# One add in place of two accumulations: spectral products of a long convolution summed on VectorE and GpSimd instead of TensorE

## The chip, the cores and the metric

The kernel runs on one core of a Trainium2 chip. The metric is the device time of one execution in microseconds; of several runs the median is given. A core has five engines that work side by side, each through its own list of instructions in order: TensorE (PE in the profile, its weight loads PEld) for matmuls, VectorE (DVE), ScalarE (ACT), GpSimd (POOL), and SyncE (SP), which here issues all DMAs. Matmul results land in PSUM, eight banks of 128x512 f32; all else lives in SBUF.

## The reference

All inputs are bf16; S is 2048 positions, D is 512 channels, F is 1792.

```python
# A: long convolution with a gate, on qn = layernorm(q)
k_shift = sum over 4 taps of shifted k * shift_k        # short causal convolution
kv      = k_shift * v
y       = irfft(rfft(pad(kv)) * rfft(pad(ssm_k)))[:S]   # causal convolution over all 2048 positions
h       = q + qn * (y + kv * ssm_D)
# B: a block with two layernorm stages, on x = layernorm(h)
g       = gelu(layernorm(x) @ w1), its four channel quarters shifted by +1, -1, +2, -2 positions
x1      = x + g @ w2
out     = h + x1 + gelu(layernorm(x1) @ w3) @ w4
```

## The kernel before, in words

**Halves and blocks.** The positions are cut into two halves, s = 0 and 1, of 8 blocks b of 128 rows; pairs p of blocks go together through the block's matmuls. The convolution is made by transforms that are written as matmuls in two steps. A signal's first step is S1 (`step1`, line 389) and its copy out of PSUM E1; eight DMAs X (line 405) then reorder it between partitions; the second step is S2 (line 413) with its copy E2. There are four signals: F0 and F1, the two halves of the filter, and A0 and A1, the two halves of kv. For F1, E2 isn't a copy but a fold: VectorE adds and subtracts F0's spectrum (line 425). kv itself comes from K (matmuls with diagonal matrices of the taps, line 442) and KV (VectorE multiplies by v, line 450). The diagonal matrices, one per channel group c, are made by `dg`, lines 296 to 309, on VectorE as four scalings of an identity or on GpSimd as one select.

**The products and the way back**, `conv(s, prods)`, from line 465. For each k of 0 to 3 (`kl`) a spectral product P(s, k, i, x) is one VectorE multiply of 128x2048 bf16 (line 474); i counts the pairs of signals, x the two forms of a complex product. Then I2(s, k, .), 16 matmuls (line 484), takes a product back one step; EV copies the four banks out, XI sends them through a DMA, and I1 (line 502) is the last step back. The first half has one pair of signals, A0 with F0: two products and two I2 for each k. The second half has two pairs, A0 with F1 and A1 with F0: four products and four I2 for each k, all accumulating in the same four banks.

**Behind it.** H (line 616) makes h from I1's banks, with the normalized q (Y, lines 611 and 613, from the statistics Q, QV, QP, QN of q), HS its statistics, uw, rr, hn the factors, hb the normalized block, LT and TE its transposition, W and U the matmul with w1 and its gelu, X2 (line 722) the matmul with w2, S (line 725) the sum x1, R a sum for the end, SS, ux, r1, xn, lb, LX, EX the same for the second layernorm, M and G (lines 777 and 781) the matmul with w3 and its gelu, O (line 790) the matmul with w4, Z the last sum, OUT the store. Some block pairs are transposed by two DMA writes and one DMA transpose, the others on TensorE; the list `BYDMA` says which.

**What sets the order.** Every step is entered with `plan.add`: a name, the engines that it may run on with a cost for each, what it depends on, and the buffers that it takes and drops. The string `ORDER` then gives the whole schedule: each word has a step's number, the letter of its engine (P, V, A, G, S for SyncE; M for two joined ScalarE copies) and the numbers of the slots that it takes, PSUM banks among them. The steps are emitted in this order, so it fixes each engine's list. An engine waits where a step's input or slot isn't ready, and everything behind it in that list waits too. Products take two of eight slots in `prs`.

In the order before, the second half's convolution stands among the first half's W, X2, M and O: I2 of k = 0 behind W of the last pair, k = 1 behind M of pair 1, k = 2 and 3 among M of pair 0, then O.0.1, O.0.0 and I1 of the second half. Here X.s.b stands for step X of half s and block b, P.1.k.i.x for a product of the second half.

Of the kernel before, what the change touches and what calls it, by code (L numbers as in the profile page):

```python
# [9 lines left out]
P = 128  # L10
# [21 lines left out]
004S 029P0 000S 002S 003S 005S 008S 031V 037V 001S 030P 063P23 006S 055P45 009S 057P67 064V 007S 056A 038G 065P01 010S 058A 019S 059P45 033V 045G  # L32
061P23 060A 087P60 039G 036V 062A 095P71 046V 042V 066A 093P4 032G 043V 047A 074S 101P5 044A 034G 015S 094V 051P23 022S 088V 053P01 035G 023S 052A
040V 072S 089P4 024S 054A 049G 091P6 021S 090V 073S 041A 097P2 096V 050G 070S 092V 099P3 048A 069S 102V 068S 107P01 098V 109P67 017S 100V 108A 103P45
067S 110V 111P23 018S 104A 115P01 071S 113P67 112A 323V 105P45 324V 116A 211P20 106V 114A 117P01 212V 119S 118A 084P4567 326V 085A 081P2301 123S 329V
086V 120S 083A 215P4 020S 082A 330V 124S 078P0167 327V 125S 217P5 080A 216V 121S 079A 075P2367 012S 218V 011S 325V 076A 127P4501 016S 319V 328V 122S
077A 219P21 129V 126S 331G 128A 013S 220V 130P6701 139V01 132A 141V23 131A 133P4501 332G 134A 140P23670 147V45 142P 135A 333G 149V67 143A 337G0
148P45011 155V01 150P 343G1 144A 145S 221P2 340G2 157V23 152A 146S 334G3 014S 151A 136P6701 222V 137V 138A 156P23452 153S 158P 154S 163V45 225P0 159A
223P1 160A 165V67 161S 164P67230 162S 226V 166P 224V 175P45 167A 168V 213P0 176A 169S 183P67 214V 170S 185P23 184A 187P45 315S 186V 177P01 188A 189P67
178V 179P23 190A 181P45 180V 171P67 028S 182A 172P01 338V 192S 231P45 196S 335V 339A 349G0 173P23 316S 344V 336A 346G3 193S 341V 235P67 232A 355G1  # L40
195S 347V 174P10 236A 352G2 191S 350V 237P45 198S 358G 342A 356V 202P6723 197S 348A 353V 194S 345A 359G 204V 239P01 238A 371G 203V 241P23 240A 227P45
242A 229P01 372G 360V 228V 230A 199P6723 247S 361G0 373V 233P45 351A 364G1 200V 362P00 234A 374G2 365P1 384V 366A 377G3 208P6745 245S 363V 354A 375P11
243S 201V 385G 367P0 376A 244S 357A 378P1 386V 246S 369P2 379A 390V0 318S 209V 397G 387A1 382P3 248S 370A 250S 388P12 210V 368A 398G 391P6 249S 380P7
383A 389A 027S 392V 399G 251P2345 263V01 381A 393P0 253A 026S 400G3 265V23 395P1 025S 252A 317S 403V2 205P6745 396A 267V45 401P23 394A 404P3 502P1
402A 206V 405A 506P0 503V 408P2 507V 504A 406P3 269V67 508A 409A 264P67011 558V 407A 266P 207V 268P 559G 270P 560G 498P2 271A 272V 561G1 510P3 564G0
499V 274S 494P4 501V 273S 562P50 511V 565P6 514P7 563A 495V 566A 411V 254P0123 496A 567P50 515V 256A 275V01 569P4 568A 577P6 277V23 570A 257P2345 578A
412V 573P7 259A 255V 571P6 258A 279V45 579P4 572A 574A 281V67 575P5 580A 516A 276P01232 414V 500A 278P 513V 280P 576A 615G 512V 282P 581P6 505V 283A
616G 517V 284A 617G 413V 621G3 287V01 618A2 619P71 587G 622P4 582V 260P0123 620V 583S 584P5 623V 588G 262A 289V23 589G 291V45 591A1 590G0 293V67
624P40 593S 261V 636P6 592S 625A 634P7 416V 509V 288P23010 635A 594S2 290P 299V01 292P 285S 294P 301V23 628P4 296A 632P7 303V45 629A 298S 637A 626P0
286S 633A 305V67 630P1 295A 410V 627A 297S 300P67231 417V 631A 302P 415V 304P 306P 418V 641P4 307A 419G 308A 309S 310S 420V 421V0 427G3 638P0 424G1  # L50
430V2 585V 642V 497V 311P16 639V 312P72 640S 422V 643S 313P35 425V 423A 433G0 428V 314P40 426A 431V 439A3 595P10 445G 442V1 432A 603P2 436V2 429A 437V
597P6 596A 434V 446G 605P7 598A 438A 447V 599P1 448V2 435A 451G3 322V 458V 607P5 600A 470V 459G 449P33 452P6 601P1 450V 453A 471G 460V 604A 440V 454P6
602A 472G 441V 461A2 456P3 443V 474G1 462A3 444V 473G0 608A 476S 606A 612P2 482V 475S 457A 463S 483G 464S 609P1 484V 477S0 485A1 486G0 455A 487S 321V
488S 465S1 518P0 522P3 489S2 480P4 523V 478P5 519V 524A 468P3 520A 481A 466P7 644V 521V 645G 490P6 467A 525V 646G 469A 492P0 610V 320G 479A 647V2
534P3 491A 648V3 649S 493A 650S 542P4 535V 554P5 537V 536A 538P3 651S3 555V 546P7 543V 556A 586S 545V 526P1 544A 611S 539V 530P6 547V 540A 550P3 527V
672G 652P00 529V 531V 658P1 673G 528V 656P5 659A 674V 532V 653A 675G1 662P4 657A 549V 676G0 660P7 551V 678S 654P5 552V 661A 677S 664P3 553V 655A 756G
548A 533V 663A 679S0 700V 665A 666P6 701G 702V 703V3 704G2 613V 669P7 757G 667V 706S 705S 541V 758G 557V 759G0 728G 680P10 729G 686P0 681A 730V 731V1
682P5 732G2 670V 687A 688P4 684P3 707S1 760G3 689A 692P2 668S 761S 693A 733S 685A 734S 708P60 714P4 735S2 712P1 720P0 671S 713A 762S 710P2 721A 715A
716P3 711A 736P10 683A 763S3 717A 742P0 709A 614S 737A 748P6 743A 738P4 749A 764P50 772P7 776P6 774P2 777A 765A 766P3 775A 768P6 767A 773A 744P5 769A
740P1 770P0 741A 739A 771A 778P2 718P4 779V 780S 719A 725P3 722P4 726V 727S 781P7 723V 724S 690P4 782V 783S 691A 697P6 745A 694P7 746P1 695V 698V 696S  # L60
747A 750P0 699S 753P2 751V 752S 754V 755S
# [32 lines left out]
def body(ctx, tc, fx, kt, q, v, sd, w1, w2, w3, w4, out):  # L94
# [200 lines left out]
    def dg(c):  # L295
        def f(e, sl):
            if e == GP:
                tap = r_k[:, c * KW + NB * 129:(c + 1) * KW].rearrange("p (j x) -> p j x", x=2)[:, :, 1:2]
                pool.affine_select(out=diag[:, c], in_=tap.to_broadcast([P, 4, P]), compare_op=OP.is_equal, fill=0.0, base=0,
                                   pattern=[[0, 4], [-1, P]], channel_multiplier=1)  # L300
                return
            for j in range(4):
                sc = r_k[:, c * KW + NB * 129:(c + 1) * KW].rearrange("p (o x) -> p o x", o=1)[:, 0, :].bitcast(F32)[:, j:j + 1]
                if e == A:
                    act.activation(diag[:, c, j, :], ident[:], ACT.Copy, scale=sc)
                else:
                    vec.tensor_scalar(out=diag[:, c, j, :], in0=ident[:], scalar1=sc, scalar2=None, op0=MUL)  # L307
# [155 lines left out]
    last_p = []  # L463

    def conv(s, prods):
        for kl in range(4):
            n = ("I2", s, kl, 0)
            for i, (a, g) in enumerate(prods):
                for x in range(2):
                    before = last_p[-1:]  # L470

# [7 lines left out]
                    def f(e, sl, i=i, x=x, kl=kl, n=n, first=first, last=last):  # L479
                        bk = got(n)  # L480
                        for xx in range(2):
                            for t in range(2):
                                for h in range(4):
                                    nc.tensor.matmul(ps[64 * t:64 * t + 64, bk[h], :], lhsT=ttab[32 * h:32 * h + 32, 2 * kl + t, 2 if x else xx, :],  # L484
                                                     rhs=prs[32 * h:32 * h + 32, got(("P", s, kl, i, x))[t], xx, :],
                                                     start=first and xx == 0, stop=last and xx == 1)
                    add(("I2", s, kl, 2 * i + x), {PEc: 0.44}, f,
                        ["tt"] + [("E2", y, kl, t) for ag in prods for y in ag for t in range(2)] if first else [("I2", s, kl, 2 * i + x - 1)],
                        take=[("ps", -2), ("vs", 1)] if first else [], drop=[(("P", s, kl, i, x), 0)], mode=3)
            for hp in range(2):  # L490
                add(("EV", s, kl, hp), EV, lambda e, sl, hp=hp, n=n: copy(e, vst[:, got(n, "vs")[0], 2 * hp:2 * hp + wide(e), :], pair(got(n), hp, wide(e))),
                    [("I2", s, kl, 2 * len(prods) - 1)], drop=[(n, hp)], mate=None if hp else (("EV", s, kl, 1), n, 0, n, 2))
# [12 lines left out]
    def qstat(s, b):  # L505
        return lambda e, sl: vec.bn_stats(qst[:, 8 * s + b, :], q_sb[:, s, b, :])
# [337 lines left out]
```

## Time and profile before

| | us |
|---|---|
| median of 3 runs | 214.38 (212.96 to 215.33) |
| the profiled execution | 213.26 |
| its span | 211.6 |
| TensorE busy | 195.7 |
| VectorE busy | 144.8 |
| ScalarE busy | 125.5 |
| GpSimd busy | 80.1 |
| VectorE, 24 spectral products (line 474) | 28.7, 1.24 each |
| TensorE, 384 matmuls of I2 (line 484) | 13.3 |
| 16 DMAs of XI, each to landing (median) | 3.9 |

The span is that of the instructions in the profile; the execution's time has 1.7 us more around it. Durations of neighbouring instructions overlap a little in the listing, so where many of one kind follow each other, the distance from start to start is the better price (six products in 7.12 us, so 1.19). A busy engine isn't yet the bound: the page gives its share in 40 slices of the span, and the chain that ended last tells where it was waited for. The granted clock of TensorE is 1.0 throughout.

### The profile page before, as it was taken

Reading aid. Unit: us, or ns where it says so; the run is one execution under the profiler, and the core shown is the slowest. Engines: PE = TensorE matmul, PEld = TensorE weight load, DVE = VectorE, ACT = ScalarE, POOL = GpSimd, SP = SyncE. Lnnn points to the kernel's source line nnn. Section 1 sums busy time; section 2 is a strip of 40 time slices with the busy share of each in tenths; the row PEclk is TensorE's granted clock in tenths of the full one; section 3 lists DMA queues with packets and bytes.
Section 4 is the critical chain, followed back from the end, with each engine's and each line's share of the span. In section 5 each row is a group of like instructions: output and inputs, shape, how many; then the busy total and the mean of one; then the engine's idle time right before and its main releaser. Section 6 shows DMA issues by size and latency. Waiting matters only on the chain.

```text
span 211.6 us, 5040 instructions
## 1 busy us (share of the span) xinstructions
PE 195.7 (93%) x1964; PEld 116.2 (55%) x1980; DVE 144.8 (68%) x302; ACT 125.5 (59%) x206; POOL 80.1 (38%) x177
## 2 busy tenths in 40 slices
PE   6899769898889999979999999989999999999992
PEld 5454323442248546636744884645848888645450
DVE  6998999999999999999868971559972000112031
ACT  3979989787999658943751883364623565301010
POOL 7850059804888140287044683212765000000000
PEclk9999999999999999999999999999999999999999
DMA  6999895976948995000693008533146440010011
GB/s 173 313 403 397 321 325 222 256 205 237 371 169 294 332 435 147 0 28 13 89 232 92 27 22 181 98 69 82 42 107 154 102 74 0 3 50 34 16 50 50
DMA packets 30809, 32.86 MB, mean 155 GB/s; under 512 B 20545, under 2 KB 22594, under 8 KB 30530
## 3 DMA queue, kind: packets, MB, share of 16 engines
q1 hardware_dynamic: 30786, 32.55, 50.8%
q8 instruction: 15, 0.25, 0.5%
q14 instruction: 8, 0.07, 0.1%
HBM read 13.14 MB, written 4.46 MB: 83 GB/s over the span
## 4 chain that ended last, share of the span: by engine, by line
PE 59%; DVE 13%; ACT 12%; DMA 6%; issue 3%; POOL 3%; SPq 3%; DVEq 0%; ACTq 0%; POOLq 0%
PE ps L777 21%; PE ps L790 18%; ACT r_a L257 5%; PE ps L722 5%; PE ps L699 5%; PE ps L484 3%; DVE r_v L616 3%; DMA r_dg<-dhb 2%; DMA r_a<-r_a 2%; PE ps L502 2%; PE ps L413 2%; DMA r_k<-in_kt_dram 2%; DVE r_f L425 2%; DVE r_dg L307 1%; DVE r_p L474 1%
## 5 line engine op out<-in xcount | busy, mean ns | idle before, releaser
L777 PEld LDWEIGHTS <-r_k 128*128 128x128 bf16 x448 | 43.5, 98 | 7.7 <-issue 1.2
L792 DVE TENSOR_TENSOR r_v<-ps,r_v 128x512 bf16<-128x512 f32 x16 | 10.7, 686 | 42.4 <-PE ps L790 42.4
L474 DVE TENSOR_TENSOR r_p<-r_a,r_f 128x2048 bf16<-128x2048 bf16 x24 | 28.7, 1240 | 1.0 <-PE ps L484 0.6
L777 PE MATMUL ps<-r_dg,r_k 128*128 128x256 bf16 x224 | 25.6, 273 | 0.1
L257 ACT CAST r_a<-ps 128x1024 bf16<-128x1024 f32 x23 | 22.2, 1026 | 3.0 <-PE ps L413 2.8
L781 ACT ACTIVATE r_f<-ps 128x512 bf16<-128x512 f32 x14 | 7.8, 599 | 20.6 <-PE ps L777 20.6
L613 POOL TENSOR_SCALAR z_t<-r_q,qrs,qnm 128x512 f32<-128x512 bf16 x11 | 13.0, 1188 | 12.6 <-DVE r_v L616 12.0
L442 PE MATMUL ps<-r_dg,r_k 128*128 128x256 bf16 (+3 forms) x108 | 15.2, 284 | 1.6 <-ACT r_f L257 0.8
L257 ACT CAST r_vs<-ps 128x1024 bf16<-128x1024 f32 x14 | 13.7, 1032 | 4.9 <-PE ps L484 4.9
L725 DVE SCALAR_TENSOR_TENSOR r_q<-r_v,hrr,ps 128x512 bf16<-128x512 bf16 x16 | 11.4, 742 | 5.9 <-PE ps L722 3.7
L781 ACT ACTIVATE r_a<-ps 128x512 bf16<-128x512 f32 x14 | 7.8, 606 | 12.2 <-PE ps L777 12.2
L257 ACT CAST r_f<-ps 128x1024 bf16<-128x1024 f32 x14 | 13.2, 1023 | 3.0 <-PE ps L389 2.8
L442 PEld LDWEIGHTS <-r_k 128*128 128x128 bf16 x112 | 9.5, 98 | 9.5 <-issue 4.8
L484 PE MATMUL ps<-r_p,ttab 32*64 32x512 bf16 x384 | 13.3, 379 | 1.0 <-DVE r_p L474 0.8
L699 PEld LDWEIGHTS <-r_fx 128*128 128x128 bf16 x128 | 12.3, 98 | 3.2 <-DMA r_dg<-dhb 0.6
L600 ACT ACTIVATE junk<-r_v 128x512 bf16<-128x512 bf16 x14 | 8.9, 635 | 7.3 <-DVE r_v L616 7.1
L777 PE MATMUL ps<-xtx,r_k 128*128 128x256 bf16 x112 | 13.0, 273 | 0.0
L600 ACT ACTIVATE junk<-r_q 128x512 bf16<-128x512 bf16 x12 | 7.6, 630 | 9.2 <-DVE r_q L725 9.1
L777 PE MATMUL ps<-xty,r_k 128*128 128x256 bf16 x112 | 12.7, 272 | 0.0
L790 PE MATMUL ps<-w4s,r_f 128*128 128x512 bf16 x54 | 12.5, 379 | 0.1
L748 POOL TENSOR_TENSOR xrr<-xrr,mhalf 128x2 f32<-128x2 f32 x8 | 7.2, 900 | 14.2 <-DVE xrr L745 13.8
L389 PEld LDWEIGHTS <-f 128*32 128x32 bf16 x256 | 6.1, 95 | 11.3 <-issue 7.5
(183 smaller groups left out, 374.7 us busy)
## 6 DMA issues: line engine op xcount, KB each, us to landing
r_z<-r_vs SPq DMA_DIRECT2D x16, 256.0 KB, 3.9
r_k<-in_kt_dram SPq DMA_DIRECT2D x8, 260.0 KB, 4.6
r_v<-in_v_dram SPq DMA_DIRECT2D x4, 512.0 KB, 7.3
r_f<-r_f SPq DMA_DIRECT2D x8, 256.0 KB, 5.2
r_q<-in_q_dram SPq DMA_DIRECT2D x8, 256.0 KB, 5.7
r_a<-r_a SPq DMA_DIRECT2D x8, 256.0 KB, 4.2
r_f<-r_a SPq DMA_DIRECT2D x8, 256.0 KB, 4.2
r_a<-r_z SPq DMA_DIRECT2D x8, 256.0 KB, 4.1
```

What stands on the lines that cost most here:

```text
L257: (act.copy if e in "AM" else on[e].tensor_copy)(o, i)
L442: nc.tensor.matmul(o[:, (d + j0) * P:(d + j1 + 1) * P], lhsT=kT[s][c][:, bb, x:x + P], rhs=diag[:, c, j0:j1 + 1, :].rearrange("p j x -> p ...
L474: on[e].tensor_tensor(out=prs[:, sl[0]:sl[0] + 2, :, :], in0=sp[a][:, kl, :, :, :], in1=gv, op=MUL)
L484: nc.tensor.matmul(ps[64 * t:64 * t + 64, bk[h], :], lhsT=ttab[32 * h:32 * h + 32, 2 * kl + t, 2 if x else xx, :], rhs=prs[32 * h:32 * h + ...
L600: act.activation(junk[:], x, ACT.Square, accum_out=sq[:, i, 1:2])
L613: on[e].tensor_scalar(out=z_t[:, sl[0], :], in0=qs, scalar1=qrs[:, i:i + 1], scalar2=qnm[:, i:i + 1], op0=MUL, op1=ADD)
L699: nc.tensor.matmul(ps[:, sl[0], j * 256:(j + 1) * 256], lhsT=w1s[:, k, m * P:(m + 1) * P], rhs=xt[:, k, :], start=(k == 0), stop=(k == DC ...
L725: vec.scalar_tensor_tensor(out=q_sb[:, s, b, :], in0=h_sb[s][:, b, :], scalar=hrr[:, 4 * s + b // 2, 0, b % 2:b % 2 + 1], in1=ps[:, got((" ...
L777: nc.tensor.matmul(ps[:, sl[0], j * 256:(j + 1) * 256], lhsT=w3s[:, k, fc * P:(fc + 1) * P], rhs=xt[:, k, :], start=(k == 0), stop=(k == D ...
L781: act.activation(gb[:, 2 * fp:2 * fp + 2, :], ps[:, got(("M", s, p, fp))[0], :].rearrange("p (j x) -> p j x", j=2), ACT.Gelu_apprx_tanh)
L790: nc.tensor.matmul(ps[:, sl[0], :], lhsT=gb[:, fc, (b % 2) * P:(b % 2 + 1) * P], rhs=w4s[:, fc, :], start=(fc == 0), stop=(fc == FC - 1))
L792: add(("Z", s, b), {V: 0.61}, lambda e, sl, b=b: vec.tensor_tensor(out=h_sb[s][:, b, :], in0=ps[:, got(("O", s, b))[0], :], in1=h_sb[s][:, ...
```

## The change

It has five parts.

1. **Sums of products.** In the second half, for each k and x, the two products (i = 0 and 1) are added elementwise by a new step PA, in place in the slots of the first product, on VectorE or GpSimd. I2 is then run on the sum alone: two I2 of 16 matmuls for each k in place of four. The first half is as before. A product no longer waits for the product entered before it.
2. **Diagonals.** `dg` has only its GpSimd form.
3. **Statistics of q.** For blocks 4 to 7 of the second half, Q moves from VectorE to ScalarE: two passes with a sum each, of q and of its square; QV has three more small instructions to bring both forms together.
4. **A new order** of all steps, with other engines for some of them. Of the eight adds, PA.1.0.0, PA.1.2.0 and PA.1.3.0 are on GpSimd, the other five on VectorE. All four `dg` are on GpSimd (two before); f2v and dr, GpSimd's before, are on VectorE; QV of the second half goes from VectorE to GpSimd.
5. `BYDMA` stays: the same block pairs are transposed by DMA.

Some stretches of the new order around the adds, engine by engine:

```
VectorE  P.1.0.0.1 P.1.0.0.0 P.1.0.1.1 P.1.0.1.0 E2.F1.2.1 S.0.2 S.0.3 PA.1.0.1 P.1.1.0.0 E2.F1.2.0 S.0.1 S.0.5 SS.0.5 EX.0.3
         S.0.0 S.0.4 P.1.1.0.1 P.1.2.0.0 R.0.4 R.0.1 P.1.1.1.1 PA.1.1.1 P.1.1.1.0 PA.1.1.0 P.1.2.1.1 EX.0.0 Q.1.1 Q.1.0
         P.1.2.0.1 P.1.2.1.0 R.0.2 lb.0.4 lb.0.5 Q.1.2 E2.A1.3.0 PA.1.2.1 P.1.3.1.0 P.1.3.0.0 P.1.3.1.1 P.1.3.0.1 PA.1.3.1 Q.1.3
GpSimd   hb.0.6 hb.0.7 PA.1.0.0 ux.0.1 r1.0.1 xn.0.1 lb.0.2 ux.0.0 r1.0.0 xn.0.0 lb.0.0 lb.0.1 ux.0.2 r1.0.2 xn.0.2
         PA.1.2.0 PA.1.3.0 edge1 QV.1 QP.1 Y.1.2
TensorE  S2.F1.2 LT.0.7 X2.0.2 X2.0.3 W.0.3.0 W.0.3.1 I2.1.0.0 I2.1.0.1 X2.0.1 X2.0.5 X2.0.4 LX.0.2 LX.0.3 X2.0.0 S2.A1.1
         six M of pair 1, S2.A1.2 M.0.1.6 O.0.2 LX.0.0 LX.0.1 I2.1.1.0 I2.1.1.1 O.0.3 S2.A1.3 six M of pair 0
         I2.1.2.0 I2.1.2.1 M.0.0.5 O.0.1 I2.1.3.0 I2.1.3.1 O.0.0 M.0.2.0 M.0.2.1 M.0.2.2 I1.1.0
```

The diff without the order and without the lines that only make room for a new block:

```diff
@@ dg @@
-            if e == GP:
-                tap = ...
-                pool.affine_select(out=diag[:, c], ...)
-                return
-            for j in range(4):
...
+            tap = ...
+            pool.affine_select(out=diag[:, c], ...)
-        add(("dg", c), {V: 0.8, A: 1.19, GP: 0.85}, dg(c), [("Lk", 0, c)], port="VG")
+        add(("dg", c), {GP: 0.65}, dg(c), [("Lk", 0, c)], port="VG")
@@ conv @@
-                    add(("P", s, kl, i, x), {V: 1.15}, f, [("E2", y, kl, t) for y in (a, g) for t in range(2)] + ["f2"] + before, take=[("pr", -1)], port="VG")
-                    last_p.append(("P", s, kl, i, x))
-                    first, last = (i, x) == (0, 0), (i, x) == (len(prods) - 1, 1)
+                    add(("P", s, kl, i, x), {V: 1.15}, f, [("E2", y, kl, t) for y in (a, g) for t in range(2)] + ["f2", "tt"], take=[("pr", -1)], port="VG")
+                    first, last, y = x == 0, x == 1, ("P", s, kl, 0, x)
+                    if i < len(prods) - 1:
+                        continue
+                    if i:
+                        def f(e, sl, x=x, kl=kl):
+                            pa, pb = (prs[:, got(("P", s, kl, j, x))[0]:got(("P", s, kl, j, x))[0] + 2, :, :] for j in range(2))
+                            on[e].tensor_tensor(out=pa, in0=pa, in1=pb, op=ADD)
+                        add(("PA", s, kl, x), {V: 1.135, GP: 3.0}, f, [y, ("P", s, kl, i, x)], drop=[(("P", s, kl, i, x), 0)], port="VG")
+                        y = ("PA", s, kl, x)
...
-                                                     rhs=prs[32 * h:32 * h + 32, got(("P", s, kl, i, x))[t], xx, :],
+                                                     rhs=prs[32 * h:32 * h + 32, got(("P", s, kl, 0, x))[t], xx, :],
...
-                    add(("I2", s, kl, 2 * i + x), {PEc: 0.44}, f,
-                        ["tt"] + [("E2", y, kl, t) for ag in prods for y in ag for t in range(2)] if first else [("I2", s, kl, 2 * i + x - 1)],
-                        take=[("ps", -2), ("vs", 1)] if first else [], drop=[(("P", s, kl, i, x), 0)], mode=3)
+                    add(("I2", s, kl, x), {PEc: 0.44}, f, [y] if first else [y, ("I2", s, kl, 0)],
+                        take=[("ps", -2), ("vs", 1)] if first else [], drop=[(("P", s, kl, 0, x), 0)], mode=3)
@@ qstat @@
+        if s == 0 or b < 4:
+            return lambda e, sl: vec.bn_stats(qst[:, 8 * s + b, :], q_sb[:, s, b, :])
+        def f(e, sl):
+            act.activation(junk[:], q_sb[:, s, b, :], ACT.Identity, accum_out=qst[:, 8 * s + b, 0:1])
+            act.activation(junk[:], q_sb[:, s, b, :], ACT.Square, accum_out=qst[:, 8 * s + b, 1:2])
+        return f
@@ qvar @@
+            if s:
+                j = slice(12, 16)
+                en.tensor_scalar(out=qmv[:, j, 0], in0=qst[:, j, 0], scalar1=1.0 / D, scalar2=0.0, op0=MUL, op1=ADD)
+                en.tensor_tensor(out=qrs[:, j], in0=qmv[:, j, 0], in1=qst[:, j, 0], op=MUL)
+                en.tensor_tensor(out=qsd[:, j], in0=qst[:, j, 1], in1=qrs[:, j], op=SUB)
+                i = slice(8, 16)
@@ steps of q @@
-            add(("Q", s, b), {V: 0.6}, qstat(s, b), [("Lq", s, b // 2)])
+            add(("Q", s, b), {A: 1.3} if s and b > 3 else {V: 0.6}, qstat(s, b), [("Lq", s, b // 2)])
```

More of the change, by code (lines that the diff above doesn't have):

```diff
@@ L505, in qstat @@
     def qstat(s, b):
-        return lambda e, sl: vec.bn_stats(qst[:, 8 * s + b, :], q_sb[:, s, b, :])
+        if s == 0 or b < 4:
[4 more added lines that the diff above has]
+        return f
     def qvar(s):
-        i = slice(8 * s, 8 * s + 8)
         def f(e, sl):
             en = on[e]
+            i = slice(8 * s, 8 * s + (4 if s else 8))
             m0, v0, m1, v1 = (qst[:, i, k] for k in (1, 2, 4, 5))
```

77 lines of the change are left out of this document (35 added, 42 removed).

## The prediction

> **What bounds the kernel now.** I read the page's first two parts, then the chain that ended last, then the timelines of single engines. The page says that TensorE (PE) is nearly always busy, that its clock is never lowered, and that VectorE (DVE) is full too until slice 20, at 106 us:
>
> ```profile
> PE 195.7 (93%) x1964; PEld 116.2 (55%) x1980; DVE 144.8 (68%) x302; ACT 125.5 (59%) x206; POOL 80.1 (38%) x177
> PE   6899769898889999979999999989999999999992
> DVE  6998999999999999999868971559972000112031
> PEclk9999999999999999999999999999999999999999
> ```
>
> The chain, in order of time, splits the span. Up to 48.5 us it changes hands between DMA, VectorE and ScalarE. From 62 to 208 us it is TensorE almost without a break, and the steps that the change shortens (L484, the step back I2 of the second half) lie on it, 64 matmuls at a time:
>
> ```profile
> 73.80 1.86 PE ps L484 x64
> 100.39 1.86 PE ps L484 x64
> 102.26 3.60 PE ps L777 x32
> 105.86 1.87 PE ps L484 x64
> 113.92 3.61 PE ps L502 x16
> ```
>
> So between the first I1 (L502, 48.50) and the last I2 (ends 107.73) two engines are full side by side. I summed the steps of each engine's list over this stretch, by start-to-start spacings from the timelines. On TensorE: S1 0.485, I1 0.945, transposes of a block 0.22, W 0.875, S2 0.57, X2 0.87, I2 0.467, M 0.89, O 3.0. This gives 53.0 us of work in 59.2, so 6.2 us of gaps and waits, most of it before 62 us. On VectorE: H, S and R 0.67, folds E2 of F1 1.2, casts 1.13, product P 1.16, Q 0.60, HS and SS 0.85. From the first H (49.66) to the last P (ends 105.67) it is 54.3 us of work in 56.0, 1.7 us of waits. VectorE has no more room than TensorE.
>
> **Part 1, fewer matmuls.** Each k of the second half has four I2 steps of 16 matmuls, 1.86 us; two remain. Gone: 4 x 0.93 = 3.7 us, all on the path above. This is the whole possible gain of the edit itself.
>
> **Part 2, the adds on VectorE.** Five of the eight adds (PA) run there. An add has the shape and type of P, so 1.16 each, 5.8 us. My list for the new order, first H to last add, has 54.0 us against 54.3: the five adds, three statistics instead of one (1.7), a Y, two lb and one more copy of a transposed block (9.0 in all) stand against three casts, two Q, two R, two hb, Z, uw, ux and two hn gone (9.3). VectorE is no lighter while TensorE is lighter by 3.7 us: it becomes the bound of this stretch.
>
> **Part 3, the adds on GpSimd.** PA.1.0.0, PA.1.2.0 and PA.1.3.0 go there, 128x2048 bf16 with two inputs. No row shows that. From below: a one-input 128x512 op takes 0.757 us undisturbed (four in 3.03), so 3.0 for four times the size. Two-input rows: f2 with 256 elements 0.61, dr with 512 elements 1.21. With 0.195 for the smallest op as fixed part they give 3.55 and 4.27; f2 scaled without it gives 4.9, the upper end. I take 4.0, between the two nearest rows.
>
> The second price is that the two engines hold each other up:
>
> ```profile
> 34.31 3.73 POOL L613 TENSOR_SCALAR z_t<-r_q,qrs,qnm 128x512 f32<-128x512 bf16 x1
> 32.92 4.63 DVE L474 TENSOR_TENSOR r_p<-r_a,r_f 128x2048 bf16<-128x2048 bf16 x4
> 50.52 3.03 POOL L613 TENSOR_SCALAR z_t<-r_q,qrs,qnm 128x512 f32<-128x512 bf16 x4 [9.15 <-DVE r_v L616]
> 66.81 2.84 POOL L655 TENSOR_SCALAR nbx<-r_v,hrr,hnm 128x512 bf16<-128x512 bf16 x1
> 69.01 0.79 DVE L655 TENSOR_SCALAR nbx<-r_v,hrr,hnm 128x512 bf16<-128x512 bf16 x1
> ```
>
> The same GpSimd step takes 0.757 beside VectorE's H (which reads PSUM) and 3.73 beside a run of products, ending half a microsecond after that run; the products keep their 1.16. At 69.01 it is VectorE that waits: its step takes 0.79, not the 0.41 of its like, until GpSimd's of 66.81 ends. So whoever is in first goes through, and a GpSimd add delays VectorE's products and adds, but not its steps that read PSUM.
>
> [...]
>
> With times counted from the first I1, and 4.0 + 0.1 per GpSimd add:
> - PA.1.0.0: VectorE ends P.1.0.1.0 at 1.16 + 20.7 + 0.6 of waits = 22.5. GpSimd adds until 26.6. VectorE meanwhile does a fold and two S (2.5), then its own add waits 1.6 and ends at 27.8; the second I2 ends at 28.3. Behind the add in GpSimd's queue stand ux, r1, xn and lb of the pair, about 3 us (rows 1.1, 0.7, 0.4, 0.77); three X2 and the two I2 cover them on TensorE.
> - From there VectorE's list holds 29.6 to PA.1.3.1. lb.0.0 and lb.0.1, on GpSimd, come beside a row of nine two-input VectorE steps and will wait as z_t did; VectorE then waits for them at EX.0.0, about 1.2. (Before, TensorE lost 1.1 at this place, to one nbx of 1.85.)
> - PA.1.2.0 gets in at Q.1.2; with the cast behind it 1.7 lie beside, so VectorE's next add waits 2.4.
> - PA.1.3.0 has only two products and an add of the same k beside it. If VectorE is first, it starts after them; if GpSimd is first, they start after it. Either way 4.1 more.
> - Sum: 27.8 + 29.6 + 1.2 + 2.4 + 4.1 = 65.1, with one I2 65.5. Before: 59.2. So the last I2 comes 6.3 us later.
>
> What TensorE has left then is less: O.0.1 (3.0) was moved ahead of the last two I2, so 96.3 against 99.3. That pays back 3.0.
>
> **Part 4, the start.** The scaling of the diagonals leaves VectorE (two dg, eight instructions, 3.14 us on the chain) for GpSimd, where two of them took 0.64 each; f2v and dr come to VectorE, dr with a wait for its DMA as late as before (8.3 us). The first gain is eaten at once: eight K steps of 0.98 and S1 on TensorE reach the A0 transforms at 16.5 in both orders. Afterwards the transfers of A0 have 1.3 MB less ahead of them on SP's queue (9.7 for 11.0 MB; Lf.1, Lv.1.0, Lk.1.2 now follow them), VectorE's list to the last product of the first half is 22.6 for 23.2 us, ScalarE's 24.4 for 23.7. VectorE had 1.6 us of waits here. I take the first I1 at 47.4 for 48.5: 1.1 gained, bounds 0 and 1.7. Q.0.0 and Q.0.1 now follow the first two products, so GpSimd's QV to Y run beside products, but end by some 40, before H needs them.
>
> **Part 5, the rest.** Four statistics of q go from VectorE (0.60) to ScalarE, two passes each with their accumulators, about 1.5: with the other moves ScalarE's list in the middle grows from 45.1 to 51.7 us, in some 60. Between 90 and 110 it was idle for 1.3 to 3 of each 5 us, which hides it; without that cover it costs gelus, and with them TensorE, up to 2 us. QV.1 on GpSimd, eleven small steps behind PA.1.3.0, ends with QP and QN about 5.5 after it; O.0.0, three M and I1 (6.6) cover that. From 113.9 on TensorE's work is the same; one transposition by DMA made it wait 0.7 at 135, and I leave it so.
>
> **The sum.** +6.3 - 3.0 - 1.1 = +2.2 us. The profiled execution took 213.26 (span 211.6 and 1.7 around it), so 215.5. The median shown is 214.38, 1.1 above it; a median after should lie so too: **216.6**, with 215.0 to 218.5 for this case.
>
> **How else it could go.**
> - *The adds lie beside.* If GpSimd's adds take 3.0 or less beside VectorE's work, TensorE sets the time: 58.5 to the last I2 instead of 59.2, 3.0 less behind it, up to 1.1 from the start, so -3.7 to -4.8 and 209.6 to 210.7. For it: only 38% of GpSimd is used. Against it: 3.73 for 0.757. [...] Chance 0.28 for clearly faster, 0.13 for a draw near 214.4.
> - *GpSimd starves further.* An add of 4.8 gives +4.6, so 219.0; ScalarE's load could do about the same. For it: f2 scaled. Against: f2's fixed part. Chance 0.21.
> - *The change doesn't do what it says:* if the order left the sums to TensorE, nothing would go; it shows eight I2 gone and eight adds, so this has no chance of its own.
> - My forecast has 0.38.
>
> Within 1% is about what a measurement of this kernel can tell from no change: 212.2 to 216.5. The forecast falls half on either side of 216.5, the draw inside. So faster 0.28, same 0.31, slower 0.41. The range reaches from the cheap adds to the dear ones, 210.0 to 219.5.
>
> **What would show it.** The three GpSimd adds near 4 us or longer, VectorE's adds of k 0 and k 2 starting only as they end, TensorE idle before I2 of k 0 and of k 3 (2 and 5 us), 256 instead of 384 matmuls in I2's line, the first I1 near 47.4. Wrong would be: GpSimd adds of 3 us or less, products running through beside them, or a wait of over 1 us behind 115 us that I didn't count.

## The result

The changed kernel takes 223.17 us (median of 5 runs, 222.88 to 224.25); the kernel before, beside it on the same chip, 214.21 (212.96 to 215.33). The ratio is 1.0435, with a 95% interval from 1.0382 to 1.0488: 4.4% slower. The forecast was 216.6 with a range up to 219.5. The side was that of the forecast; the time lies outside its range.

The span of the profiled execution is 221.4 us, for 211.6 before. Parts 1 and 2 of its page (busy time of each engine, busy tenths in 40 slices of 5.5 us, granted clock):

```profile
PE 197.1 (89%) x1852; PEld 116.1 (52%) x1852; DVE 157.9 (71%) x299; ACT 131.7 (59%) x218; POOL 100.2 (45%) x195
PE   7999678898878889979848999979999999999993
DVE  6899999789997899999999598377988200022121
PEclk9999969999999999999995999999999999999999
```

TensorE has 112 matmul records fewer, and yet it is busy 1.4 us longer. VectorE is busy 13 us longer, most of it, as will be seen, in steps that are held up. And the last line, all nines before, has a 6 in slice 5 (27.7 to 33.2 us) and a 5 in slice 21 (116.2 to 121.8).

The chain that ended last, in order of time (start, duration, engine, what it writes, line). L470 is the new add PA, L479 is I2 (L484 before), L462 the product P (L474), L661 the normalized blocks, L796 is O (L790):

```profile
72.99 4.03 POOL r_p L470
...
92.45 3.46 POOL nbx L661 x2
...
96.35 1.00 PE ps L479 x32
...
107.52 8.50 DVE r_p L462 x4
...
117.31 1.08 PE ps L479 x14
118.39 4.91 PE ps L796 x14
```

Before, this stretch was TensorE almost without a break. Now GpSimd and VectorE hand the chain to each other. Three instants place the loss: the first I1 starts at 49.09 (before 48.50), the last I2 ends at 118.39 (before 107.73), and the span ends 103.0 us behind that (before 103.9). So of the 9.8 us of span, 0.6 are lost ahead of the first I1, 10.1 between it and the last I2, and 0.9 are won back behind.

How the 10.1 come about is seen in the timelines (start, duration, engine, line, operation). GpSimd first; the row of 69.46 is two steps hb, that of 99.49 the end of xn.0.2, the others are the three adds:

```profile
69.46 3.53 POOL L661 TENSOR_SCALAR nbx<-r_v,hrr,hnm 128x512 bf16<-128x512 bf16 x2
72.96 4.06 POOL L470 TENSOR_TENSOR r_p<-r_p 128x2048 bf16<-128x2048 bf16 x1
...
99.49 0.58 POOL L762 TENSOR_TENSOR xnm<-xnm,xrr 128x2 f32<-128x2 f32 x1
100.03 4.05 POOL L470 TENSOR_TENSOR r_p<-r_p 128x2048 bf16<-128x2048 bf16 x1
...
110.02 4.90 POOL L470 TENSOR_TENSOR r_p<-r_p 128x2048 bf16<-128x2048 bf16 x1 [5.94 <-DVE r_p L462]
```

VectorE at the same times:

```profile
75.96 2.14 DVE L470 TENSOR_TENSOR r_p<-r_p 128x2048 bf16<-128x2048 bf16 x1
100.10 4.45 DVE L661 TENSOR_SCALAR r_k<-r_q,xrr,xnm 128x512 bf16<-128x512 bf16 x2
107.52 8.49 DVE L462 TENSOR_TENSOR r_p<-r_a,r_f 128x2048 bf16<-128x2048 bf16 x4
```

Its own add at 75.96 takes 2.14, and ends a microsecond after GpSimd's; undisturbed adds take 1.14 to 1.23. The two lb of 100.10, one-input steps on small tiles, take 4.45; two such took 0.73 in experiment 1. The four products at 107.52 take 8.49, where four took 4.63 before. So VectorE stood for 1.0 + 3.7 + 3.9 = 8.6 us while GpSimd added.

TensorE at the third add, in windows of half a microsecond (window, length, busy time and matmuls, granted clock, DMA share, GB/s):

```profile
112.00:112.50 0.50, 0.37 (x2) 1.00 1.08 225
112.50:113.00 0.50, 0.00 (x0) 1.00 1.06 258
...
114.50:115.00 0.50, 0.03 (x8) 1.00 1.06 213
115.00:115.50 0.50, 0.50 (x16) 0.64 0.91 213
...
121.50:122.00 0.50, 0.50 (x2) 0.53 0.53 184
122.00:122.50 0.50, 0.50 (x4) 1.00 0.78 180
```

TensorE stands from 112.4 to 115.0. Worked out from the shares 0.64 and 0.53, its clock is granted at half from 115.14 to 121.97, for 6.8 us, though TensorE works without a break from 117.3 on.

### The profile page after: what moved, and what is told of

It is laid out like the page before. It is cut to its first block, busy times and chain, and to the rows that moved or that the text cites. A ratio compares the mean times of both kernels' runs of the same rounds, so it can differ in the third digit from the quotient of the medians.

```text
span 221.4 us, 4839 instructions
## 1 busy us (share of the span) xinstructions
PE 197.1 (89%) x1852; PEld 116.1 (52%) x1852; DVE 157.9 (71%) x299; ACT 131.7 (59%) x218; POOL 100.2 (45%) x195
## 3 DMA queue, kind: packets, MB, share of 16 engines
q1 hardware_dynamic: 30786, 32.55, 48.9%
## 4 chain that ended last, share of the span: by engine, by line
PE 49%; POOL 13%; DVE 12%; issue 3%; DMA 2%; ACT 0%; DVEq 0%; POOLq 0%; ACTq 0%
PE ps L796 20%; PE ps L783 17%; DVE r_p L462 4%; PE ps L728 4%; POOL nbx L661 3%; PE ps L705 3%; DVE r_f L417 2%; DMA xtx<-dhb 2%; DVE r_v L622 2%; PE ps L496 2%; POOL r_p L470 2%; PE ps L434 1%; PE ps L381 1%; PE ps L479 1%; DVE r_p L470 1%
## 5 line engine op out<-in xcount | busy, mean ns | idle before, releaser
L462 DVE TENSOR_TENSOR r_p<-r_a,r_f 128x2048 bf16<-128x2048 bf16 x24 | 32.8, 1406 | 1.7 <-ACT r_a L257 1.1
L257 ACT CAST r_a<-ps 128x1024 bf16<-128x1024 f32 x26 | 25.0, 1023 | 5.7 <-PE ps L405 3.5
L479 PE MATMUL ps<-r_p,ttab 32*64 32x512 bf16 x256 | 11.3, 438 | 5.7 <-POOL r_p L470 2.8
L470 POOL TENSOR_TENSOR r_p<-r_p 128x2048 bf16<-128x2048 bf16 x3 | 13.0, 4336 | 5.9 <-DVE r_p L462 5.9
L796 PE MATMUL ps<-w4s,r_v 128*128 128x512 bf16 x56 | 14.5, 418 | 0.0
L787 ACT ACTIVATE r_kv<-ps 128x512 bf16<-128x512 f32 x14 | 7.8, 596 | 10.0 <-PE ps L783 10.0
L619 POOL TENSOR_SCALAR z_t<-r_q,qrs,qnm 128x512 f32<-128x512 bf16 x9 | 9.5, 1060 | 8.7 <-DVE r_v L622 7.1
L796 PE MATMUL ps<-w4s,r_kv 128*128 128x512 bf16 x56 | 12.6, 379 | 0.0
L622 DVE SCALAR_TENSOR_TENSOR r_v<-ps,qsd,z_t 128x512 bf16<-128x512 f32 x16 | 11.1, 745 | 1.9 <-PE ps L496 1.9
```

The costliest lines, as they stand in the source:

```text
L257: (act.copy if e in "AM" else on[e].tensor_copy)(o, i)
L462: on[e].tensor_tensor(out=prs[:, sl[0]:sl[0] + 2, :, :], in0=sp[a][:, kl, :, :, :], in1=gv, op=MUL)
L470: on[e].tensor_tensor(out=pa, in0=pa, in1=pb, op=ADD)
L622: vec.scalar_tensor_tensor(out=h_sb[s][:, b, :], in0=ps[:, got(("I1", s, b // 2))[b % 2], :], scalar=qsd[:, i:i + 1], in1=z_t[:, got(("Y", ...
L787: act.activation(gb[:, 2 * fp:2 * fp + 2, :], ps[:, got(("M", s, p, fp))[0], :].rearrange("p (j x) -> p j x", j=2), ACT.Gelu_apprx_tanh)
L796: nc.tensor.matmul(ps[:, sl[0], :], lhsT=gb[:, fc, (b % 2) * P:(b % 2 + 1) * P], rhs=w4s[:, fc, :], start=(fc == 0), stop=(fc == FC - 1))
```

## The experiments

Each ratio is to the kernel before, run on the same chip beside it; 1% is 2.1 us. Instants of a profile are given as first I1 / end of the last I2 / span: 48.50 / 107.7 / 211.6 before, 49.09 / 118.4 / 221.4 after. The theories: **A**, the three adds on GpSimd are the loss, because the two engines shut each other out. **B**, VectorE's list is the bound of the stretch, whoever adds. **D**, formed after the first runs: GpSimd's queue, late with other steps, holds the transposes of the blocks.

### 1. The three adds on VectorE

The changed kernel with PA.1.0.0, PA.1.2.0 and PA.1.3.0 on VectorE at the same places of the order.

```diff
- ... 266G ... 290G ... 302G ...
+ ... 266V ... 290V ... 302V ...
```

> The changed kernel with its three GpSimd adds on VectorE, at the same places of the order. Theory A (the three adds on GpSimd hold up VectorE and, through it, TensorE): VectorE no longer stands blocked (1.0 us at its own add of k 0, 3.8 at lb.0.4, 3.9 in the products of k 3, together 8.7) and does three more adds of 1.16 (3.5); with the lowered TensorE clock after the wait of k 3 gone too, 5 to 8 us faster than the changed kernel: 215 to 218. Rival B (VectorE has simply too much to do, wherever the adds are): 3.5 us more on VectorE, so 223 to 227. Rival C (the rest of the new order is what costs): no change, 222 to 224.

Measured 215.66 (215.0 to 217.29), ratio 1.0039 [1.0004, 1.0074]; 49.1 / 111.8 / 213.9. VectorE's timeline at the places of the long rows:

```profile
99.23 0.73 DVE L660 TENSOR_SCALAR r_k<-r_q,xrr,xnm 128x512 bf16<-128x512 bf16 x2
...
104.06 2.36 DVE L461 TENSOR_TENSOR r_p<-r_a,r_f 128x2048 bf16<-128x2048 bf16 x2
```

None of these steps is held up any more, and the clock stays at 1.0 in this stretch. 7.5 of the 9.0 us of the medians (8.5 by the ratios) were the three adds being on GpSimd, although VectorE's list got 3.5 us longer. That the loss comes from the three adds being on GpSimd is shown by this run. How it comes about is read from the rows: VectorE is shut out (two lb took 4.45 for 0.73), and a GpSimd add is also over three times as long as one on VectorE (4.05 for 1.23). At k = 3 the add started at 110.02, and its undisturbed 4.05 alone would, as an estimate, end it at 114.1; its I2 started at 114.97. So a part of the loss is the add's own length, and no run separates the two. It is left open, too, why nothing is gained.

### 2. The clock kept up

The changed kernel, with 9 and 4 matmuls that nobody reads ahead of the two I2 of k = 3, into a free PSUM bank.

```diff
+for i in range((9, 4)[x] if (s, kl) == (1, 3) else 0):
+    nc.tensor.matmul(ps[:, 1, :], lhsT=w4s[:, 0, 0:P], rhs=w4s[:, 1, :], start=True, stop=True)
```

> The changed kernel with 13 extra matmuls of 128x512 in two places where TensorE stood idle: nine ahead of the first and four ahead of the second I2 of k 3, into a PSUM bank that is free there; their result is overwritten. Theory E (after the wait of 2.6 us TensorE's granted clock falls to 0.5 for some 6 us, and that, not the wait, costs 2.4 us of the 9: O.0.0 took 4.9 instead of 3.0): with TensorE busy the clock stays up, 220.5 to 221.5. Rival F (the clock fell for another reason, or the filling is on the path): 223 to 225.

Measured 221.57 (220.12 to 222.76), ratio 1.0333 [1.0285, 1.0382]; 48.1 / 117.1 / 218.4. The same step O.0.0 in TensorE's timeline, first of the changed kernel:

```profile
118.33 4.97 PE L796 MATMUL ps<-w4s,r_v 128*128 128x512 bf16 x14
```

and here:

```profile
117.11 2.97 PE L798 MATMUL ps<-w4s,r_v 128*128 128x512 bf16 x13 [0.16 <-issue]
```

The granted clock is 1.00 throughout from 107.5 to 125 us. The half clock behind the wait of k = 3 costs 0.0102 of the time, 2.2 us; the intervals of the two ratios just touch. The two rows agree with 2.0 us, and so do the profiles: from the first I1 to the end it is 172.3 us in the changed kernel and 170.3 here (the first I1 is 1.0 earlier here, which the added matmuls, behind it, can't have done). The rest of the 8.5 us, about 6.3, is what the GpSimd adds cost otherwise: VectorE shut out, and their own length.

### 3. The adds in the old order

The kernel before with the changed convolution, all eight adds on VectorE, each right behind its second product, the rest of the order as before.

```diff
- ... 264V01 ... 265V23 ... 264P67011 ... 266P ...
+ ... 264V01 ... 265V45 266V ... 267P67011 ...
```

> The kernel before with the sums alone: all eight adds on VectorE, each right behind its second product, two steps I2 for each k where the last two of four stood; order, diagonals and statistics as before. If VectorE is as full as TensorE in this stretch (theory A and rival B): 9.3 us more on VectorE less its 1.7 of waits there, TensorE's 3.7 saved for nothing: 219 to 222. If the saved matmuls are on the path and VectorE has room (rival C, the new order is the fault): 210 to 212.

Measured 225.88 (224.68 to 227.45), ratio 1.0492 [1.0427, 1.0558]; 51.2 / 121.2 / 225.7. More than expected. I2 of k = 2 waits in TensorE's timeline:

```profile
112.55 1.93 PE L486 MATMUL ps<-r_p,ttab 32*64 32x512 bf16 x32 [5.25 <-DVE r_p L469]
```

and again the clock falls during the wait (windows as above):

```profile
111.00:111.50 0.50, 0.00 (x0) 0.71 0.18 41
111.50:112.00 0.50, 0.00 (x0) 0.50 1.18 270
...
117.50:118.00 0.50, 0.50 (x4) 0.50 1.03 381
118.00:118.50 0.50, 0.50 (x7) 0.97 1.16 266
```

Eight adds are 9.3 us on a full VectorE, without any GpSimd add. So the new order isn't what makes the change slow: with all adds on VectorE it is 10 us faster than the old one, one reason being, by the lists, that it takes casts and other steps off VectorE. VectorE is busy 66.2 of the 70.0 us from the first I1 to the last I2, which speaks for its list as the bound in the old order. But not all of the 11.2 us is the list. The profiled execution, the slowest of the four, has its first I1 2.7 later than before, ahead of every add, and the last I2 another 10.7 later. Its clock is at half in three stretches, 32.7 to 39.5, 80.5 to 83.9 and 111.2 to 118.0 us, 17.1 us in all, and VectorE waits 2.06 for slots. The shares of adds and clock weren't separated.

### 4. Is it VectorE's list in the new order?

First the three GpSimd adds left out altogether (the second products are missing in these three sums), everything else as changed:

```diff
+if e == GP:
+    return
 on[e].tensor_tensor(out=pa, in0=pa, in1=pb, op=ADD)
```

> The changed kernel with the three GpSimd adds left out (the second products of these three sums are not added). It prices the three adds as a whole. Theory A: VectorE gains the 8.7 us for which it stood blocked, TensorE its full clock: 212 to 215. Rival B: VectorE's load is the same as in the changed kernel, so less than 2 us: 221 to 223. Rival C: 221 to 224.

Measured 215.5 (213.59 to 217.28), ratio 1.0041 [0.9998, 1.0083]; 49.9 / 112.3 / 214.0. No faster than experiment 1, which has 3.5 us more on VectorE: against theory B by itself. TensorE's waits from 46 to 120 us (line, what it waits for: total, times, longest), the two largest:

```profile
PE ps L678 <- POOL nbx L663: 2.7, 3, 1.3
PE ps L405 <- DMA r_a<-r_z: 1.3, 1, 1.3
```

They point to theory D, and to transfers behind it. So experiment 1 again, with seven steps (ux.0.0, ux.0.1, xn.0.0, lb.0.0, lb.0.1, hb.0.5, hb.0.7) moved from GpSimd to VectorE:

```diff
- ... 390G0 ... 403G2 ... 558G ... 615G ... 617G ... 618G3 ... 621G2 ...
+ ... 390V0 ... 403V2 ... 558V ... 615V ... 617V ... 618V3 ... 621V2 ...
```

> The kernel of e1 (all eight adds on VectorE) with seven more GpSimd steps on VectorE: ux of pairs 1 and 0, xn, lb.0.0 and lb.0.1 of pair 0, hb.0.5 and hb.0.7. In e1 TensorE waited 3.0 us for blocks that GpSimd made late beside VectorE's two-input instructions (0.9 before LT.0.7, 0.5 before LX.0.2, 0.3 and 1.3 before LX.0.0 and LX.0.1). Theory D (in e1 the saved 3.7 us of matmuls are lost in TensorE's waits for GpSimd, which VectorE's products shut out): these waits go, 2 to 3 us faster than e1: 212.5 to 214. Rival B (VectorE's list decides): 2.8 us more on VectorE, so 216 to 218.5.

Measured 215.94 (214.92 to 218.08), ratio 1.0083 [1.0047, 1.012]; 48.9 / 111.9 / 214.1. TensorE's largest wait from 76 to 120 us is now

```profile
PE ps L478 <- DVE r_p L469: 2.1, 3, 1.2
```

The waits for GpSimd are gone but for 0.2, those for VectorE have taken their place, and nothing is gained. D falls as the one cause. A further run put S2.A1.0, which waits for a transfer, behind W.0.2.1 on TensorE:

```diff
- ... 251P6745 250S ... 253A 395P3 ...
+ ... 250S ... 395P3 251P6745 253A ...
```

> The kernel of e5 with S2 of A1, k 0, two W steps later in TensorE's list; in e1 TensorE stood 1.4 us before it, waiting for the DMAs of A1, with W.0.1.0 and W.0.2.1 behind it ready. Theory D, extended (each wait of TensorE in this stretch counts): 0.8 to 1.4 us faster than e5: 211.5 to 213. Rival B: no change or 0.5 slower than e5, because VectorE's products of A1 come later: 213 to 219.

Measured 217.97 (216.22 to 219.04), ratio 1.015 [1.0101, 1.02]; 49.6 / 113.9 / 216.3. Two microseconds slower by the medians, though the two intervals overlap. In the profiles I2 of k = 0 starts at 77.3 for 75.6; 0.7 of that is a later first I1, and the rest goes with the second half's spectrum and VectorE's products, which came later. Removing the wait for the transfer gained nothing.

Then both at once, the queue relieved and the three adds not computed:

```diff
+if (kl, x) in ((0, 0), (2, 0), (3, 0)):
+    return
 on[e].tensor_tensor(out=pa, in0=pa, in1=pb, op=ADD)
```

> The version with all adds on VectorE and GpSimd's queue relieved by seven steps, with PA.1.0.0, PA.1.2.0 and PA.1.3.0 not computed at all (their second products are missing in the result). This takes 3.5 us off VectorE's list where GpSimd is no longer waited for. Theory B (two limits at once: VectorE's list when GpSimd is relieved, GpSimd's late blocks when VectorE is): with both relieved the saved matmuls show; last I2 at about 109 instead of 111.9, time 212.5 to 213.5, ratio 0.987 to 0.994 of the version before the change. Rival: a third limit (transfers, or TensorE's own order) holds the stretch: 215 to 216 again, waits of TensorE for VectorE replaced by waits for DMA.

Measured 213.57 (212.48 to 215.58), ratio 0.9967 [0.9927, 1.0008]; 48.9 / 111.1 / 212.6. Each alone gained nothing; both together gain 2.5 us against the relieved queue alone, and 1.5 against experiment 1, where the intervals just touch. That fits two limits at once, GpSimd's late blocks and VectorE's list. But the last I2 comes at 111.1, not at the expected 109, and 213.6 is still not 210. Between 52 and 76 us TensorE waits for a block from GpSimd (the row below), and 2.4 us in all for transfers:

```profile
PE ps L677 <- POOL nbx L662: 1.7, 1, 1.7
```

So GpSimd's late blocks weren't fully removed as a limit, and the waits for transfers stand beside both.

### 5. What the saved matmuls are worth

No adds at all, in the old order (experiment 3 without them) and in the new (experiment 1 without them):

```diff
+return
-on[e].tensor_tensor(out=pa, in0=pa, in1=pb, op=ADD)
```

> The kernel before with the changed convolution and none of the eight adds computed (the second products of the second half are missing in the result): its old order, eight I2 fewer, VectorE's and GpSimd's lists as before the change. What the saved matmuls are worth by themselves. If TensorE bounds the stretch in the old order: 3.7 us less, 210.5 to 211, ratio 0.983. If VectorE's list (54.3 us in 56.0) bounds it just as much: the wait of I2 for products takes the place of the matmuls, 213.5 to 214.5.

> The changed kernel with none of the eight adds computed (the same products missing). VectorE's list is 5.8 us shorter than in the changed kernel, and GpSimd has none of the three long steps. If the new order loses the saving before the first add, between 52 and 76 us, where TensorE idles 3.5 us more than before in every version with this order (transfers in front of the second transform steps, the late normalized block on GpSimd): 213 to 213.7, no better than the version with three adds left out and the queue relieved, and 2 to 3 us above the old order without adds. If the adds are what eats the saving: 210.5 to 211.5, level with the old order without adds.

The old order measured 214.54 (213.47 to 216.03), ratio 1.0018 [0.9987, 1.0048]; 48.7 / 107.5 / 211.8. The new order measured 212.88 (211.75 to 215.77), ratio 0.9925 [0.9897, 0.9954]; 49.0 / 109.2 / 211.0. Three windows of TensorE (as above), first of the kernel before:

```profile
48.00:76.00 28.00, 25.66 (x329) 1.00 0.81 293
76.00:100.00 24.00, 22.76 (x246) 1.00 0.28 98
100.00:126.00 26.00, 25.80 (x288) 1.00 0.45 92
```

then of the old order without adds:

```profile
48.00:76.00 28.00, 25.70 (x306) 1.00 0.77 271
76.00:100.00 24.00, 21.69 (x211) 1.00 0.35 125
100.00:126.00 26.00, 24.29 (x226) 1.00 0.44 92
```

and of the new order without adds:

```profile
48.00:76.00 28.00, 23.01 (x278) 1.00 0.75 260
76.00:100.00 24.00, 23.54 (x254) 1.00 0.39 137
100.00:126.00 26.00, 25.53 (x221) 1.00 0.39 102
```

In the old order TensorE is busy 71.7 of these 78 us for 74.2, and the span is the same: idle time took the place of the matmuls. Three waits of TensorE are new or longer (rows of its timeline; the first is the transposition of a block that ScalarE normalizes, whose wait was 0.39 before; the second is I2 of k = 2, the third the I1 behind the transfer that follows the last I2; the latter two had no such wait before):

```profile
92.81 0.40 PE L671 MATMUL ps<-ident,nbx 128*128 128x128 bf16 x4 [1.25 <-ACT nbx L654]
...
101.82 1.07 PE L486 MATMUL ps<-r_p,ttab 32*64 32x512 bf16 x32 [1.21 <-DVE r_p L469]
...
113.99 3.61 PE L503 MATMUL ps<-r_z,f 128*128 128x512 bf16 x16 [0.34 <-DMA r_z<-r_vs]
```

So even adds at no price gain nothing in the old order. Part of the saving goes into a wait for VectorE's product, as the expectation's second branch has it, and part into ScalarE's block and the transfer, which it hadn't named. VectorE's list, on which the adds would stand, is one of the limits beside TensorE, not the only one.

In the new order even free adds gain only 1.6 us. TensorE idles 5.0 us between 48 and 76 us, for 2.3 before; that is ahead of nearly all adds (the first stands at 73 in the changed kernel). TensorE's largest waits there are for transfers in front of S2 (1.8 for F1's, 1.2 for A1's; before 0.3 and none) and 0.8 for a block from GpSimd. The chain of this run goes, in this stretch and the next, through GpSimd and ScalarE too (L660 the normalized blocks; L503 and L504 the statistics of q that the change put on ScalarE):

```profile
69.14 3.53 POOL nbx L660 x2
...
90.87 0.62 ACT junk L503 x2
91.51 0.73 ACT junk L504 x2
```

The expectation offered 213 to 213.7 for a loss by the new order and 210.5 to 211.5 for one by the adds; 212.9 lies at the edge of the first. But it put the old order without adds at 2 to 3 us below the new, and that is reversed. It is neither the order nor the adds alone: in either order the saved time goes into other waits, for transfers and GpSimd's block in the new, for ScalarE's block, VectorE's product and a transfer in the old.

### 6. The other parts by themselves

The kernel before with the four dg on GpSimd and Q.1.4 to Q.1.7 on ScalarE; then with the dg alone.

```diff
- ... 033V ... 036V ... 414V ... 415V ... 416V ... 417V ...
+ ... 033G ... 036G ... 414A ... 415A ... 416A ... 417A ...
```

> The kernel before with the other two parts alone: all four diagonals on GpSimd, and the four statistics of the second half on ScalarE, at their old places in the order; products and I2 as before. Theory A and rival B: these parts cost or gain next to nothing, 213 to 215. Rival C, if it is these parts that cost: 217 or more.

> The kernel before with all four diagonals on GpSimd and nothing else, to split e4 (plus 1.3 us for diagonals and statistics together). If the diagonals do it (GpSimd's selects stand ahead of the table steps, and hold up VectorE's): 215 to 216. If ScalarE's statistics do it: 214 to 214.8.

Measured 216.48 (214.89 to 219.21), ratio 1.0063 [1.0023, 1.0103], and 214.91 (213.81 to 216.83), ratio 1.0032 [0.9993, 1.0071]. The diagonals cost nothing that can be told from no change, and gain nothing. With the statistics it is some 1.3 us slower than before; in its profile TensorE's wait for a block from ScalarE grows from 0.4 to 2.2 us. The two runs can't be told from each other by their intervals.

### 7. A try to do better

Three residual sums (R.0.1, R.0.2, R.0.4; 0.67 each) that stood among the products moved behind the last add, once with GpSimd's queue relieved and once without.

```diff
- ... 513V ... 501V ... 505V ... 305V ... 642V ...
+ ... 305V 501V ... 642V 513V 505V ...
```

> A complete kernel: all adds on VectorE, GpSimd's queue relieved by seven steps, and three residual sums R.0.1, R.0.4, R.0.2 (0.67 each, VectorE), which only the final sums need, moved from among the products to behind the last add. If VectorE's list is the limit there: 2.0 us earlier last I2 (about 110), time 213.5 to 214.2, level with the kernel before or just below. If the list isn't the limit: 215.5 to 216.

> All adds on VectorE, GpSimd's queue as in the changed kernel, and the same three residual sums moved behind the last add. If VectorE and GpSimd hold this stretch by turns: GpSimd's late blocks still bind, so no more than 0.5 us against 215.7, that is 215.2 to 215.7. If VectorE's list alone is the limit: 2.0 less, 213.7.

Measured 218.13 (216.36 to 220.02), ratio 1.0149 [1.0085, 1.0212], and 218.26 (216.71 to 219.71), ratio 1.017 [1.011, 1.023]. Both slower, against every expectation; against the same kernel without the move the second is clearly slower, while the first's interval overlaps that of the relieved queue. In the first the last I2 ends at 111.2, 0.7 earlier than without the move, and then TensorE waits for VectorE behind it:

```profile
116.84 1.03 PE L782 MATMUL ps<-r_dg,r_k 128*128 128x256 bf16 x8 [1.60 <-DVE r_v L797]
118.33 1.50 PE L782 MATMUL ps<-r_dg,r_k 128*128 128x256 bf16 x8 [0.45 <-DVE r_v L797]
119.62 3.15 PE L495 MATMUL ps<-r_z,f 128*128 128x512 bf16 x8
```

L797 is the final sum Z, which frees the PSUM banks that M takes next. In VectorE's list one moved sum now stands ahead of the first Z, and all three ahead of the two Z that these rows wait for; the same waits were 0.25 or less without the move. The I1 in the third row takes 3.15 us where 1.89 is usual: the granted clock is at half again, from 118.7 to 122.2, in this execution. In the profile of the second version the same two waits stand, 1.60 and 0.45, and the I1 behind them takes 1.89. No version run here that computes everything is faster than the kernel before.

## Why the prediction was wrong

**The sum, term by term.** The mechanism that the forecast named came about: GpSimd's adds take 4 us (4.06, 4.05, 4.90), they and VectorE shut each other out (VectorE stood 1.0, 3.7 and 3.9 us beside them, and two hb of GpSimd took 3.53 beside its products, for 1.53 before), and the last I2 comes later. The size was wrong. The forecast put the changed span at 213.8 (215.5 less 1.7); it is 221.4, 7.6 more. Four terms failed: the clock, put at nothing; the start, whose 1.1 didn't come; the place at which PA.1.2.0 gets in; and the two steps ahead of PA.1.0.0 that were late. By its own steps:

- *Part 2, adds on VectorE at 1.16*: right, 1.14 to 1.23.
- *Part 3, an add on GpSimd at 4.0, and the engines exclude each other*: right in kind and nearly in size (4.06, 4.05, 4.90). That VectorE's own add of k = 0 would wait 1.6 was 1.0.
- *PA.1.0.0 ends 26.6 after the first I1*: it ended at 27.9, VectorE's add behind it at 29.0 for 27.8. Two of its terms were late: VectorE's products (they waited 1.14 for the spectrum, behind S2.A1.0's wait for a transfer), and GpSimd's queue, in which the two hb of 69.46 took 3.53. I had put such a wait at lb.0.0 and lb.0.1, where it also came (3.46), but not at hb. Cost: 1.2.
- *PA.1.2.0 gets in at Q.1.2, with 1.7 of VectorE's work beside it, so 2.4 of wait*: it got in two steps earlier, ahead of lb.0.4 and lb.0.5. These need xn.0.2, and in GpSimd's list PA.1.2.0 stands right behind xn.0.2. That step ended at 100.07, GpSimd went on with the add, and VectorE's lb began at 100.10, behind it. So the two lb took 4.45, a wait of 3.7, and Q and the cast, which were to lie beside the add, came after it. The order that I had listed shows who comes first; and that a one-input VectorE step of this shape can be held was in my row of 69.01 (0.79 for 0.41). Cost: 1.3.
- *PA.1.3.0, 4.1 either way*: right, 3.9, GpSimd's add having slipped between the products.
- *The last I2 at 65.5*: it ended 69.3 after the first I1. 1.2 and 1.3 of the 3.8 are named; 0.5 is the last I2 at half clock (1.0 for 0.467), and the rest is small.
- *The clock*: not in the sum at all. I had TensorE idle for 5 us ahead of k = 3, and took the granted clock as 1.0 because the profile before shows no other value. In the changed kernel it fell to half 0.17 us after a wait of 2.60 and stayed there for 6.8. The price was measured at 2.2 us (experiment 2). The 0.5 of the last I2 belongs to it; O.0.0 with 4.9 for 3.0 is why the 3.0 for O.0.1 paid back only 0.9.
- *Part 4, the first I1 1.1 earlier*: it came 0.6 later, so 1.7 were missing. Executions with the same early order have it anywhere from 48.1 to 49.9, and the old early order gave 48.5, 48.7 and 51.2, so the runs can't tell the 0.6 from nothing; a gain isn't seen. What moves it between executions stays open; in the changed kernel the clock was at half from 29.81 to 33.22 us and in experiment 3 from 32.7 to 39.5, in the kernel before nowhere. In the profile, VectorE's early table steps ran beside GpSimd's diagonals (the first took 1.15 for 0.69), and the diagonals by themselves gave nothing in experiment 6.
- *Part 5*: the wait at a transfer grew from 0.4 to 1.3 at 146 us, which I had left as it was. That ScalarE's statistics are hidden held in the changed kernel, where they stand on no chain; in the versions without GpSimd's adds they come onto it.

These four misses (1.2, 1.3, clock about 2, start 1.7) make 6.2 of 7.6.

**The signs I named.** GpSimd adds near 4 us or more, VectorE's add of k = 0 waiting, 256 matmuls of I2, TensorE idle ahead of k = 3 (2.60 and 1.37 us in place of 5): seen. TensorE idle 2 us before I2 of k = 0: not seen, 0.16 and 0.45 only, since the steps ahead of it had been late too. The first I1 near 47.4: not seen. VectorE's add of k = 2 starting only as GpSimd's ends: not seen, the two lb stood there in its place. Of the signs of being wrong, one came: a wait of over 1 us behind 115 us that I hadn't counted, the 1.3 at 146.

**The rivals.** "The adds lie beside" had 0.28 for a gain of 3.7 to 4.8. Its condition, adds of 3.0 or less, didn't come. With adds at no price the gain was 1.6 in the new order and none in the old, so its mechanism, that TensorE then sets the time, doesn't hold either: other waits of TensorE, for transfers and blocks and in the old order for VectorE, take most of the saving. That VectorE's list was full my own sums (53.0 of 59.2, 54.3 of 56.0) had shown, and I drew the consequence for the forecast but not for the rival. By the forecast's sum, +2.2 us with three adds of 4.0, an add of 3.3 us would break even; that sum lacks these limits, and 3.3 was too high as well: adds of 1.2 on VectorE already gave no gain. "GpSimd starves further" at 219.0 was the nearest; its cause, an add of 4.8, came about in one add of three.

**The account that the runs give**, in ratios times 214.4: without adds in the new order -1.6; the eight adds on VectorE +2.4 (from 0.9925 to 1.0039); three of them moved to GpSimd +8.5 (to 1.0435), of which 2.2 are the clock. Two things remain open. One is how the 6.3 left of the 8.5 divide between VectorE being shut out and the length of the adds themselves. The other is how the missing part of the first 3.7 divides among VectorE's list, GpSimd's late blocks, ScalarE's statistics and the transfers between 48 and 76 us: removing one makes the next wait longer, and no run removed all.

## What to carry to other kernels

Before a saving on the busiest engine is counted, count the lists of the other engines in the same stretch, and the waits close behind: here 3.7 us of matmuls were worth 0 and 1.6 us with the added work left out, and the added work came on top of that. A run with the new work left out gives that ceiling. Price an operation on GpSimd with what VectorE loses beside it: here adds of 4.06, 4.05 and 4.90 us cost it 1.0, 3.7 and 3.9, and beside the first it did two S, which read PSUM, at 0.75 each. Which steps can pass must be read from rows of the same shape, and which engine gets in first from what the other engine's next step waits for. Where a forecast contains a wait of some microseconds on TensorE, price the clock behind it too: here 2.2 us behind a wait of 2.60.

## What the runs showed of the hardware

- The granted clock fell to half at 115.14 us in the changed kernel, 0.17 behind a wait of TensorE of 2.60, and at 111.2 in experiment 3, 3.9 into a wait of 5.25, and stayed there for 6.8 us in both. In the changed kernel it fell also at 29.81, 0.68 into a wait of 1.24 that came 1.28 us of work after one of 1.20, until 33.22, so for 3.41 us. A wait of TensorE doesn't settle it by its length alone: with the same two, 1.60 and 0.45, the clock was at half from 118.7 to 122.2 in one version of experiment 7, whose I1 behind them took 3.15 us, and in the other that I1 took 1.89.
- A GpSimd add with two bf16 inputs of 128x2048 took 4.05 us (100.03 in the changed kernel). Two of VectorE's one-input steps on 128x512 bf16 (lb), begun 0.07 later, took 4.45 beside it; in experiment 1, with that add on VectorE, they took 0.73.
- With thirteen matmuls that compute nothing of use the granted clock stayed at 1.00 from 107.5 to 125 us, and the kernel took 2.2 us less (ratios 1.0435 and 1.0333, whose intervals touch).
